# Scale-and-add over 16.8 MB arrays: y whole in SBUF and two large stores, in place of pooled chunks of 16 rows

## The chip, the cores and the metric

The kernel runs on one core of one Trainium2 chip. The metric is the device time of one execution in microseconds (us). The kernel before takes 123.67 us (median of 4 runs, 123.56 to 123.85). Its profiled execution has a span of 122.0 us. The measured time is about 1.7 us more than the span, because the two have different end points.

## The reference

```python
B, S, D = 1024, 16, 512                # bfloat16
x = normal(B, S, D) * 0.05
y = normal(B, S, D) * 0.05
gamma = 1e-4 * normal(D) * 0.05
def reference(x, y, gamma):
    return x + gamma * y
```

There are 16384 rows of 512 elements, 1 KB each. They are spread over 128 partitions, so each partition holds 128 consecutive rows, 128 KB of each array. x and y must be read and the result written: 3 x 16.78 = 50.33 MB.

## The kernel before

The rows are worked in chunks of 16 (the last two of 8). x and y pass through pools of 5 and 6 buffers. SP issues the loads of x, ACT those of y, and GpSimd the stores. These are three separate DMA queues. VectorE multiplies y by gamma in place and then adds x. A scheduler orders the VectorE instructions.

```python
MAIN_CHUNK = 16
TAIL_CHUNKS = [8, 8]
X_BUFS = 5
Y_BUFS = 6
...   # gamma is broadcast to 128 partitions by a matmul with ones; a pad aligns the pools to 16 KB
    for cs in chunks:
        xt = x_pool.tile([P, max_chunk, D], xf.dtype, tag="xt")
        yt = y_pool.tile([P, max_chunk, D], yf.dtype, tag="yt")
        nc.sync.dma_start(out=xt[:, :cs, :], in_=xv[:, r0 : r0 + cs, :])
        nc.scalar.dma_start(out=yt[:, :cs, :], in_=yv[:, r0 : r0 + cs, :])
        nc.vector.tensor_tensor(out=yt[:, :cs, :], in0=yt[:, :cs, :],
            in1=gamma_sb[:, None, :].to_broadcast([P, cs, D]), op=mybir.AluOpType.mult)
        nc.vector.tensor_tensor(out=yt[:, :cs, :], in0=xt[:, :cs, :], in1=yt[:, :cs, :],
            op=mybir.AluOpType.add)
        nc.gpsimd.dma_start(out=ov[:, r0 : r0 + cs, :], in_=yt[:, :cs, :])
        r0 += cs
```

Of the kernel before, what the change touches and what calls it, by code (L numbers as in the profile page):

```python
# [1 line left out]

# [4 lines left out]

MAIN_CHUNK = 16
TAIL_CHUNKS = [8, 8]
X_BUFS = 5  # L10
Y_BUFS = 6
SBUF_ALIGN = 16384
SLOT_ROUND = 32


def _chunk_schedule(n_per_part: int) -> list[int]:
    tail = [c for c in TAIL_CHUNKS if c < MAIN_CHUNK]
    rem = n_per_part - sum(tail)
    if rem < 0:
        return [1] * n_per_part  # L20
    chunks = []
    while rem >= MAIN_CHUNK:
        chunks.append(MAIN_CHUNK)
        rem -= MAIN_CHUNK
    if rem > 0:
        chunks.append(rem)
    chunks.extend(tail)
    assert sum(chunks) == n_per_part, (chunks, n_per_part)
    return chunks


def _round_up(v: int, m: int) -> int:
    return ((v + m - 1) // m) * m


@with_exitstack
def kernel(
    ctx: ExitStack,
    tc: tile.TileContext,
    x: bass.AP,  # L40
    y: bass.AP,
    gamma: bass.AP,
    out: bass.AP,
):
    nc = tc.nc
    P = nc.NUM_PARTITIONS

    xf = x.flatten_outer_dims()
    yf = y.flatten_outer_dims()
    of = out.flatten_outer_dims()  # L50
    N, D = xf.shape
    assert N % P == 0, (N, P)
    n_per_part = N // P
    gdt = gamma.dtype

    xv = xf.rearrange("(p n) d -> p n d", p=P)
    yv = yf.rearrange("(p n) d -> p n d", p=P)
    ov = of.rearrange("(p n) d -> p n d", p=P)

    chunks = _chunk_schedule(n_per_part)  # L60
    max_chunk = max(chunks)

    const_pool = ctx.enter_context(tc.tile_pool(name="const", bufs=1))
    gamma_row = const_pool.tile([1, D], gdt)
    ones_row = const_pool.tile([1, P], gdt)
    gamma_sb = const_pool.tile([P, D], gdt)
    used = nc.sbuf_base
    used = _round_up(used, SLOT_ROUND)
    for nbytes in (D * mybir.dt.size(gdt), P * mybir.dt.size(gdt), D * mybir.dt.size(gdt)):
        used += _round_up(nbytes, SLOT_ROUND)  # L70
    pad_bytes = (-used) % SBUF_ALIGN
    pad_sb = None
    if pad_bytes > 0:
        pad_sb = const_pool.tile([P, pad_bytes], mybir.dt.uint8)

    x_pool = ctx.enter_context(tc.tile_pool(name="xio", bufs=X_BUFS))
    y_pool = ctx.enter_context(tc.tile_pool(name="yio", bufs=Y_BUFS))
    psum_pool = ctx.enter_context(tc.tile_pool(name="psum", bufs=1, space=bass.MemoryType.PSUM))

    nc.gpsimd.dma_start(out=gamma_row[:], in_=gamma.unsqueeze(0))  # L80
    nc.vector.memset(ones_row[:], 1.0)  # L81
    if pad_sb is not None:
        nc.vector.memset(pad_sb[:, 0:64], 0)  # L83
    gamma_ps = psum_pool.tile([P, D], mybir.dt.float32)
    nc.tensor.matmul(gamma_ps[:], ones_row[:], gamma_row[:], start=True, stop=True)  # L85
    nc.vector.tensor_copy(out=gamma_sb[:], in_=gamma_ps[:])  # L86

    r0 = 0
    for cs in chunks:
        xt = x_pool.tile([P, max_chunk, D], xf.dtype, tag="xt")  # L90
        yt = y_pool.tile([P, max_chunk, D], yf.dtype, tag="yt")
        nc.sync.dma_start(out=xt[:, :cs, :], in_=xv[:, r0 : r0 + cs, :])
        nc.scalar.dma_start(out=yt[:, :cs, :], in_=yv[:, r0 : r0 + cs, :])  # L93
        nc.vector.tensor_tensor(  # L94
            out=yt[:, :cs, :],
            in0=yt[:, :cs, :],
            in1=gamma_sb[:, None, :].to_broadcast([P, cs, D]),
            op=mybir.AluOpType.mult,
        )
        nc.vector.tensor_tensor(  # L100
            out=yt[:, :cs, :],
            in0=xt[:, :cs, :],
            in1=yt[:, :cs, :],
            op=mybir.AluOpType.add,
        )
        nc.gpsimd.dma_start(out=ov[:, r0 : r0 + cs, :], in_=yt[:, :cs, :])  # L106
        r0 += cs
    assert r0 == n_per_part


# [1 line left out]
_INS = ['x', 'y', 'gamma']  # L112
_OUTS = [((1024, 16, 512), 'bfloat16')]


# [23 lines left out]
```

## Time and profile before

| what | value | where it is read |
|---|---|---|
| time, span | 123.67 us, 122.0 us | runs, page |
| bytes | 50.33 MB, 412 GB/s over the span | page, DMA queues |
| DMA engines busy | 32.7 + 32.7 + 32.2 = 97.6% | page, DMA queues |
| VectorE busy | 71.1 us, 58% | page, busy time |
| one VectorE operation | 4.42 us for 8192 columns, 2.29 for 4096 | groups by shape |

These lines are from the page of the kernel before. "DMA" is the busy share of the 16 engines in tenths, for 40 equal slices of 3.05 us; "GB/s" is what they moved. The three lines below are the DMA queues with packets, MB and share of the 16 engines' span: q1 is SP's queue, q10 is ACT's, q0 is GpSimd's.

```profile
...
DMA  4999999999999999999999999999999999999993
GB/s 118 424 435 430 430 430 430 430 349 435 430 430 435 435 440 430 430 430 430 430 440 435 430 430 430 430 430 430 430 397 454 413 430 419 464 430 430 397 427 126
...
q10 hardware_dynamic: 1296, 16.78, 32.7%
q1 hardware_dynamic: 1296, 16.78, 32.7%
q0 software_dynamic: 1328, 16.78, 32.2%
...
```

Every slice but the first and the last is at 9, the highest digit. The rate is about 430 GB/s both while only loads run and while stores are mixed in. The Trainium skill ("DMA: Bandwidth & Descriptors", section "Where 436 GB/s comes from") gives 435 GB/s as the ceiling of the ports; this trace agrees within 1 to 2%. So the kernel is bound by the DMA engines, and its bytes alone need 117 us at 430 GB/s.

The next lines are groups of VectorE instructions of the kernel before, with shapes kept apart: count, busy us, mean ns of one, then the idle time before them and what ended it.

```profile
...
L94 DVE TENSOR_TENSOR yt<-yt,gamma_sb 128x8192 bf16<-128x8192 bf16 x7 | 31.0, 4423 | 33.4 <-DMA yt<-in_y_dram 33.4
L100 DVE TENSOR_TENSOR yt<-xt,yt 128x8192 bf16<-128x8192 bf16 x7 | 30.7, 4419 | 0.0
...
L94 DVE TENSOR_TENSOR yt<-yt,gamma_sb 128x4096 bf16<-128x4096 bf16 x2 | 4.6, 2287 | 2.0 <-DMA yt<-in_y_dram 2.0
...
```

Here is the beginning of its timeline: start, duration, engine, line, operation, and in brackets the idle time before it.

```profile
...
13.06 4.42 DVE L94 TENSOR_TENSOR yt<-yt,gamma_sb 128x8192 bf16<-128x8192 bf16 x1 [3.82 <-DMA yt<-in_y_dram]
17.52 4.42 DVE L100 TENSOR_TENSOR yt<-xt,yt 128x8192 bf16<-128x8192 bf16 x1
22.26 0.55 POOL L106 DMA_DIRECT2D out_dram<-yt  x1 [20.38 <-DVE yt L100]
...
36.19 4.42 DVE L94 TENSOR_TENSOR yt<-yt,gamma_sb 128x8192 bf16<-128x8192 bf16 x1 [9.04 <-DMA yt<-in_y_dram]
...
```

VectorE waits for y again and again (33.4 us before the large multiplies). The first store is issued at 22.26 us, so from then on stores and loads share the engines.

### The profile page before, as it was taken

What the parts mean: (1) busy time and instruction counts of PE and PEld (TensorE: products, weight loads), DVE (VectorE), ACT (ScalarE), POOL (GpSimd) and SP (SyncE); (2) the same over time, 40 slices, a digit from 0 to 9 for tenths busy, and PEclk for the clock granted to TensorE, in tenths of its full rate; (3) what the DMA queues carried; (4) which work ended last, traced back from release to release, by engine and by line L of the source; (5) the groups of instructions that cost most, each with busy time, mean ns of one, the idle gap of its engine ahead of it and who ended that gap; (6) DMA issues with size and microseconds to landing.
All of it is one profiled execution on the core that took longest, in us unless ns stands there. A gap on an engine that the chain in (4) does not pass through costs nothing.

```text
span 122.0 us, 123 instructions
## 1 busy us (share of the span) xinstructions
PE 0.6 (0%) x1; PEld 0.1 (0%) x1; DVE 71.1 (58%) x21; POOL 5.6 (5%) x14
## 2 busy tenths in 40 slices
PE   0010000000000000000000000000000000000000
PEld 0000000000000000000000000000000000000000
DVE  0010799780019999950079995940019999859600
POOL 2000000100000010100000011000000010100300
DMA  4999999999999999999999999999999999999993
GB/s 118 424 435 430 430 430 430 430 349 435 430 430 435 435 440 430 430 430 430 430 440 435 430 430 430 430 430 430 430 397 454 413 430 419 464 430 430 397 427 126
DMA packets 3920, 50.33 MB, mean 412 GB/s; under 512 B 464, under 2 KB 464, under 8 KB 464
## 3 DMA queue, kind: packets, MB, share of 16 engines
q10 hardware_dynamic: 1296, 16.78, 32.7%
q1 hardware_dynamic: 1296, 16.78, 32.7%
q0 software_dynamic: 1328, 16.78, 32.2%
HBM read 33.56 MB, written 16.78 MB: 412 GB/s over the span
## 4 chain that ended last, share of the span: by engine, by line
DMA 66%; issue 15%; DVE 11%; POOL 1%; POOLq 0%; DVEq 0%; ACTq 0%
DMA yt<-in_y_dram 50%; DMA out_dram<-yt 16%; DVE yt L100 7%; DVE yt L94 4%; POOL out_dram L106 1%; POOLq L134 0%; DVEq L94 0%; POOLq L106 0%; ACTq L93 0%; DVEq L100 0%
## 5 line engine op out<-in xcount | busy, mean ns | idle before, releaser
L94 DVE TENSOR_TENSOR yt<-yt,gamma_sb 128x8192 bf16<-128x8192 bf16 (+1 forms) x9 | 35.5, 3949 | 35.5 <-DMA yt<-in_y_dram 35.5
L100 DVE TENSOR_TENSOR yt<-xt,yt 128x8192 bf16<-128x8192 bf16 (+1 forms) x9 | 35.2, 3944 | 0.0
L106 POOL DMA_DIRECT2D out_dram<-yt x9 | 4.8, 533 | 109.1 <-DVE yt L100 109.1
L86 DVE CAST gamma_sb<-gamma_ps 128x512 bf16<-128x512 f32 x1 | 0.7, 690 | 7.5 <-PE gamma_ps L85 7.5
L80 POOL DMA_DIRECT2D gamma_row<-in_gamma_dram x1 | 0.6, 618 | 0.8 <-POOLq L123 0.8
L81 DVE MEMSET ones_row<- 1x128 bf16 x1 | 0.2, 165 | 0.8 <-PEq L123 0.8
L85 PE MATMUL gamma_ps<-gamma_row,ones_row 1*128 1x512 bf16 x1 | 0.6, 577 | 7.9 <-DMA gamma_row<-in_gamma_dram 7.9
L123 POOL MEMSET const-float32-0.0<- 128x1 f32 x1 | 0.1, 98 | 0.2 <-issue 0.2
L123 POOL MEMSET const-bfloat16-1.0<- 128x1 bf16 x1 | 0.1, 102 | 0.0
L85 PEld LDWEIGHTS <-ones_row 1*128 1x128 bf16 x1 | 0.1, 101 | 1.0 <-DVE pad_sb L83 1.0
L123 POOL MEMSET const-float32-1.0<- 128x1 f32 x1 | 0.1, 98 | 0.0
L123 POOL MEMSET const-uint8-127<- 128x1 uint8 x1 | 0.1, 98 | 0.0
L83 DVE MEMSET pad_sb<- 128x16 uint32 x1 | 0.1, 72 | 0.0
## 6 DMA issues: line engine op xcount, KB each, us to landing
yt<-in_y_dram ACTq DMA_DIRECT2D x7, 2048.0 KB, 45.5
xt<-in_x_dram SPq DMA_DIRECT2D x7, 2048.0 KB, 45.4
out_dram<-yt POOLq DMA_DIRECT2D x7, 2048.0 KB, 19.1
xt<-in_x_dram SPq DMA_DIRECT2D x2, 1024.0 KB, 44.4
yt<-in_y_dram ACTq DMA_DIRECT2D x2, 1024.0 KB, 32.7
out_dram<-yt POOLq DMA_DIRECT2D x2, 1024.0 KB, 5.5
gamma_row<-in_gamma_dram POOLq DMA_DIRECT2D x1, 1.0 KB, 6.6
```

The costliest lines, as they stand in the source:

```text
L80: nc.gpsimd.dma_start(out=gamma_row[:], in_=gamma.unsqueeze(0))
L81: nc.vector.memset(ones_row[:], 1.0)
L83: nc.vector.memset(pad_sb[:, 0:64], 0)
L85: nc.tensor.matmul(gamma_ps[:], ones_row[:], gamma_row[:], start=True, stop=True)
L86: nc.vector.tensor_copy(out=gamma_sb[:], in_=gamma_ps[:])
L94: nc.vector.tensor_tensor(out=yt[:, :cs, :], in0=yt[:, :cs, :], in1=gamma_sb[:, None, :].to_broadcast([P, cs, D]), op=mybir.AluOpType.mult,)
L100: nc.vector.tensor_tensor(out=yt[:, :cs, :], in0=xt[:, :cs, :], in1=yt[:, :cs, :], op=mybir.AluOpType.add,)
L106: nc.gpsimd.dma_start(out=ov[:, r0 : r0 + cs, :], in_=yt[:, :cs, :])
L123: nc = _bacc.Bacc("TRN2", target_bir_lowering=False, num_devices=1)
```

## The change

The intent is fewer and larger transfers. y stays whole in SBUF (128 KB per partition), the result replaces it, and all loads of y can be issued at once. x passes through two slots of 32 rows. Two stores of 64 rows (64 KB per partition) close the program: the first on SP's queue, behind the last load of x, the second on ACT's queue, behind the last load of y. The order is the program's own; no scheduler moves anything.

```diff
-MAIN_CHUNK = 16
-TAIL_CHUNKS = [8, 8]
-X_BUFS = 5
-Y_BUFS = 6
+PIECE = 32
+X_SLOTS = 2
+STORE = 64
 ...                                  # the 16 KB alignment pad goes too
+    y_sb = y_pool.tile([P, rows, D], dt)
+    ctx.enter_context(tc.manual_schedule())
+    for c in range(n_pieces):
+        r = slice(c * PIECE, (c + 1) * PIECE)
+        xt = x_pool.tile([P, PIECE, D], dt, tag="xt")
+        yt = y_sb[:, r, :]
+        nc.sync.dma_start(out=xt[:], in_=xv[:, r, :])
+        nc.scalar.dma_start(out=yt, in_=yv[:, r, :])
 ...                                  # the same multiply and add, on 32 rows
-        nc.gpsimd.dma_start(out=ov[:, r0 : r0 + cs, :], in_=yt[:, :cs, :])
+    for c in range(rows // STORE):
+        r = slice(c * STORE, (c + 1) * STORE)
+        eng = nc.sync if c % 2 == 0 else nc.scalar
+        eng.dma_start(out=ov[:, r, :], in_=y_sb[:, r, :])
```

Below, piece 0 to 3 are the four pieces of 32 rows, and x2, y3 and so on are their loads.

More of the change, by code (lines that the diff above doesn't have):

```diff
@@ L6 @@
 from concourse._compat import with_exitstack
-MAIN_CHUNK = 16
-TAIL_CHUNKS = [8, 8]
-X_BUFS = 5
-Y_BUFS = 6
-SBUF_ALIGN = 16384
-SLOT_ROUND = 32
-def _chunk_schedule(n_per_part: int) -> list[int]:
-    tail = [c for c in TAIL_CHUNKS if c < MAIN_CHUNK]
-    rem = n_per_part - sum(tail)
-    if rem < 0:
-        return [1] * n_per_part
-    chunks = []
-    while rem >= MAIN_CHUNK:
-        chunks.append(MAIN_CHUNK)
-        rem -= MAIN_CHUNK
-    if rem > 0:
-        chunks.append(rem)
-    chunks.extend(tail)
-    assert sum(chunks) == n_per_part, (chunks, n_per_part)
-    return chunks
-def _round_up(v: int, m: int) -> int:
-    return ((v + m - 1) // m) * m
+PIECE = 32
+X_SLOTS = 2
+STORE = 64
 @with_exitstack
@@ L51 @@
     N, D = xf.shape
-    assert N % P == 0, (N, P)
-    n_per_part = N // P
-    gdt = gamma.dtype
+    rows = N // P
+    n_pieces = rows // PIECE
+    dt = xf.dtype
     xv = xf.rearrange("(p n) d -> p n d", p=P)
@@ L58 @@
     ov = of.rearrange("(p n) d -> p n d", p=P)
-    chunks = _chunk_schedule(n_per_part)
-    max_chunk = max(chunks)
     const_pool = ctx.enter_context(tc.tile_pool(name="const", bufs=1))
-    gamma_row = const_pool.tile([1, D], gdt)
-    ones_row = const_pool.tile([1, P], gdt)
-    gamma_sb = const_pool.tile([P, D], gdt)
-    used = nc.sbuf_base
-    used = _round_up(used, SLOT_ROUND)
-    for nbytes in (D * mybir.dt.size(gdt), P * mybir.dt.size(gdt), D * mybir.dt.size(gdt)):
-        used += _round_up(nbytes, SLOT_ROUND)
-    pad_bytes = (-used) % SBUF_ALIGN
-    pad_sb = None
-    if pad_bytes > 0:
-        pad_sb = const_pool.tile([P, pad_bytes], mybir.dt.uint8)
-    x_pool = ctx.enter_context(tc.tile_pool(name="xio", bufs=X_BUFS))
-    y_pool = ctx.enter_context(tc.tile_pool(name="yio", bufs=Y_BUFS))
+    gamma_row = const_pool.tile([1, D], dt)
+    ones_row = const_pool.tile([1, P], dt)
+    gamma_sb = const_pool.tile([P, D], dt)
     psum_pool = ctx.enter_context(tc.tile_pool(name="psum", bufs=1, space=bass.MemoryType.PSUM))
@@ L81 @@
     nc.vector.memset(ones_row[:], 1.0)
-    if pad_sb is not None:
-        nc.vector.memset(pad_sb[:, 0:64], 0)
     gamma_ps = psum_pool.tile([P, D], mybir.dt.float32)
@@ L86 @@
     nc.vector.tensor_copy(out=gamma_sb[:], in_=gamma_ps[:])
-    r0 = 0
-    for cs in chunks:
-        xt = x_pool.tile([P, max_chunk, D], xf.dtype, tag="xt")
-        yt = y_pool.tile([P, max_chunk, D], yf.dtype, tag="yt")
-        nc.sync.dma_start(out=xt[:, :cs, :], in_=xv[:, r0 : r0 + cs, :])
-        nc.scalar.dma_start(out=yt[:, :cs, :], in_=yv[:, r0 : r0 + cs, :])
+    y_pool = ctx.enter_context(tc.tile_pool(name="y", bufs=1))
+    x_pool = ctx.enter_context(tc.tile_pool(name="x", bufs=X_SLOTS))
+    y_sb = y_pool.tile([P, rows, D], dt)
[6 more added lines that the diff above has]
+        nc.scalar.dma_start(out=yt, in_=yv[:, r, :])
         nc.vector.tensor_tensor(
-            out=yt[:, :cs, :],
-            in0=yt[:, :cs, :],
-            in1=gamma_sb[:, None, :].to_broadcast([P, cs, D]),
+            out=yt,
+            in0=yt,
+            in1=gamma_sb[:, None, :].to_broadcast([P, PIECE, D]),
             op=mybir.AluOpType.mult,
         )
-        nc.vector.tensor_tensor(
-            out=yt[:, :cs, :],
-            in0=xt[:, :cs, :],
-            in1=yt[:, :cs, :],
-            op=mybir.AluOpType.add,
-        )
-        nc.gpsimd.dma_start(out=ov[:, r0 : r0 + cs, :], in_=yt[:, :cs, :])
-        r0 += cs
-    assert r0 == n_per_part
+        nc.vector.tensor_tensor(out=yt, in0=xt[:], in1=yt, op=mybir.AluOpType.add)
+    for c in range(rows // STORE):
+        r = slice(c * STORE, (c + 1) * STORE)
+        eng = nc.sync if c % 2 == 0 else nc.scalar
+        eng.dma_start(out=ov[:, r, :], in_=y_sb[:, r, :])
 _INS = ['x', 'y', 'gamma']
```

## The prediction

> **What bounds the kernel now.** The 16 DMA engines. The page's DMA row is 9 (of 10) in every slice except the first and the last, and the three DMA queues add up to 32.7 + 32.7 + 32.2 = 97.6% of the engines' span. 50.33 MB move at 424 to 435 GB/s in nearly all slices, loads alone (first 22 us) or mixed with stores. The Trainium skill, "DMA: Bandwidth & Descriptors", section "Where 436 GB/s comes from", gives a ceiling of 435 GB/s for the ports; this trace agrees. VectorE is busy 58% and hidden. At 430 GB/s the bytes alone need 117.0 us of the 122.0 us span. About 5 us are left: about 2.2 us before the first bytes flow (first slice: 118 GB/s), the last landing and the end, and small dips (349 and 397 GB/s slices).
>
> **What the change does.** Bytes are the same. Loads go from 2 MB to 4 MB, stores from nine (issued by GpSimd, spread over the run) to two of 8 MB (SP and ACT), both late. So the run becomes a load phase, then a store phase. The question is only whether the DMA engines ever run dry.
>
> **Estimate, from the trace's numbers** (430 GB/s; start 2.2 us; landing about 1.1 us after the last byte: the first 4 MB pair landed at 13.0 us). VectorE took 4.42 us for 8192 columns and 2.28 us for 4096, so 16384 columns should take 8.7 us, and a piece (multiply and add) 17.4 us. A piece's loads, 8.39 MB, take 19.5 us: VectorE is a little quicker than the DMA and keeps up.
> - x0, y0 land at 22.8; piece 0 done at 40.3; x2 is issued then. x1's bytes end at 41.2, so the SP queue is short of work for about 0.6 us, but y2 is already queued on ACT and fills the engines.
> - x1, y1 land at 42.3; piece 1 done at 59.8; x3 and the first store are issued then, before x2's bytes end (61.3).
> - Loads end at about 80.3; piece 2 is done at 78.9, piece 3 at about 98.
> - The first store, behind x3 in SP's queue, streams from 80 to about 99.7. The second store is issued at 98.3 and flows from about 99.6. Almost no gap, but the margin is under 1 us.
> - Last byte at about 119.5, span about 121.5.
>
> The removed GpSimd issues (9 x 0.53 us) are off the critical path: worth nothing. Lost may be: a gap of 0 to 3 us before the second store, and a slower store-only phase (slices after the last load showed 430, 397 and 427 GB/s; 3% over 40 us is 1.2 us). The skill's section "Issuing engines are not separate DMA queues" says that the issuing engine does not matter; so I expect one queue alone to fill the 16 engines. This trace does not show that.
>
> **Prediction.** Measured time is about 1.7 us over the span: 123.4 us, range 121.9 to 126.2. Faster by over 2%: 0.04; within 2%: 0.85; slower: 0.11.
>
> **What would show it.** DMA row 9 throughout; bandwidth about 430 in both phases; VectorE operations of 8.7 us; last VectorE operation ending near 98 us; the second store issued within 1 us of the first store's last byte; chain of waits: loads, then the last multiply and add, then the second store.
>
> **What would make it wrong.** A store-only phase on a single queue well below 430 GB/s (slower); 4 MB loads landing unevenly, so that piece 3 ends after the first store (slower by that gap); removal of the 16 KB alignment pad slowing transfers; or a phase of pure reads or pure writes running above 435 GB/s (faster).

## The result and the profile after

The changed kernel takes 123.38 us (median of 4 runs, 123.06 to 123.58) against 123.67 us. The ratio is 0.9973, with a 95% interval of 0.9955 to 0.9991: the same within 2%, though a 0.3% gain is clear of noise. Ratios here and below are the mean time of one kernel's fast runs over that of the other's of the same rounds, so they are not quite the ratios of the medians quoted.

The same lines of the page of the changed kernel, in slices of 3.03 us:

```profile
...
DMA  6898989899999999999999999897997799777970
GB/s 173 367 497 378 486 378 486 378 486 400 465 400 465 400 465 400 465 400 465 400 465 400 465 400 465 346 519 346 562 475 346 346 627 411 346 346 346 692 346 0
...
q1 hardware_dynamic: 720, 25.17, 49.0%
q10 hardware_dynamic: 720, 25.17, 48.3%
...
```

The engines are busy 97.3%, against 97.6% before. Here the DMA row shows digits from 7 to 9, not 9 throughout. That is no idle time: the page counts a whole packet, its bytes and its duration, in the slice in which it starts, and packets are now 32 and 64 KB. When the packet records are spread over the time that they really took, every slice but the first and the last is full to within 1%, in both kernels. GpSimd's queue now carries gamma alone. The packets fell from 3920 to 1472 (without those under 512 B, from 3456 to 1280).

The groups of VectorE operations, shapes kept apart:

```profile
...
L60 DVE TENSOR_TENSOR y_sb<-y_sb,gamma_sb 128x16384 bf16<-128x16384 bf16 x4 | 34.8, 8692 | 15.6 <-DMA y_sb<-in_y_dram 15.6
L66 DVE TENSOR_TENSOR y_sb<-xt,y_sb 128x16384 bf16<-128x16384 bf16 x4 | 34.8, 8691 | 0.1
...
```

One operation on 16384 columns takes 8.69 us (8.7 was predicted). The timeline of the changed kernel from the first load's landing on:

```profile
...
22.90 8.69 DVE L60 TENSOR_TENSOR y_sb<-y_sb,gamma_sb 128x16384 bf16<-128x16384 bf16 x1 [11.10 <-DMA y_sb<-in_y_dram]
31.62 8.69 DVE L66 TENSOR_TENSOR y_sb<-xt,y_sb 128x16384 bf16<-128x16384 bf16 x1
42.27 8.69 DVE L60 TENSOR_TENSOR y_sb<-y_sb,gamma_sb 128x16384 bf16<-128x16384 bf16 x1 [1.96 <-DMA y_sb<-in_y_dram]
51.00 8.69 DVE L66 TENSOR_TENSOR y_sb<-xt,y_sb 128x16384 bf16<-128x16384 bf16 x1
60.09 0.42 SPq L70 DMA_DIRECT2D out_dram<-y_sb  x1
60.10 8.69 DVE L60 TENSOR_TENSOR y_sb<-y_sb,gamma_sb 128x16384 bf16<-128x16384 bf16 x1 [0.41 <-DMA y_sb<-in_y_dram]
68.83 8.69 DVE L66 TENSOR_TENSOR y_sb<-xt,y_sb 128x16384 bf16<-128x16384 bf16 x1
79.61 8.69 DVE L60 TENSOR_TENSOR y_sb<-y_sb,gamma_sb 128x16384 bf16<-128x16384 bf16 x1 [2.09 <-DMA y_sb<-in_y_dram]
88.33 8.69 DVE L66 TENSOR_TENSOR y_sb<-xt,y_sb 128x16384 bf16<-128x16384 bf16 x1
97.05 0.35 ACTq L70 DMA_DIRECT2D out_dram<-y_sb  x1
...
```

Each piece starts when its y lands (22.90, 42.27, 60.10, 79.61 us) and takes 17.4 us. The last one ends at 97.02 us, and the second store is issued at 97.05. The chain that ended last, by line, in the view of the chain:

```profile
...
by line: DMA y_sb<-in_y_dram 33.9%; DVE y_sb L60 21.5%; DVE y_sb L66 21.5%; another core or an unknown queue 2.0%; ACTq L59 0.3%; issue 0.2%
...
```

This chain puts 43% of the span on VectorE. It lists one way back from the end, not what bounds the kernel: the packet records say that the engines were never dry while VectorE worked. The first experiment tests which reading is right. (The chain also does not list the second store, which ends the program at 120.2 us.)

The trace records each packet with its size and duration. I used them for an account of the span. A packet of 8, 16, 32 and 64 KB takes 0.309, 0.611, 1.213 and 2.418 us (medians) on one engine. Twice the time of one size is 7 to 9 ns more than the time of the next size, so by my estimate each packet costs about 8 ns besides its bytes. "Packets" below is count times median over 16 engines. "Start stall" is what packets in the first 5 us took beyond their median, "other" is such excess later plus the time in which engines had no packet, and "end" runs from the end of the last packet to the end of the span. All values are us; one execution each.

```
kernel        first  packets  start stall  other    end   = span
before         1.73   117.48         0.59   0.67   1.58   122.05
changed        1.75   116.32         0.65   1.08   1.48   121.29
tiny_compute   1.77   116.32         0.70   1.01   1.39   121.19
late8          1.74   116.32         0.65   8.01   1.40   128.12
one_store      1.77   116.32         0.63  18.11   1.34   138.16
four_stores    1.74   116.45         0.68   1.21   1.66   121.75
p16            1.75   117.31         0.56   0.52   1.42   121.56
p8             1.74   118.66         0.73   0.30   1.46   122.88
swap           1.75   116.32         0.62   2.97   1.46   123.11
pool_stores    1.74   116.32         0.66  14.91   1.41   135.03
pool_late      1.73   116.38         0.70   0.21   1.48   120.51
sp_three       1.73   116.38         0.73   1.04   1.48   121.37
sp_three_l8    1.74   117.86         0.58   0.70   1.57   122.44
one_slot       1.74   116.32         0.68  23.98   1.40   144.12
```

Two things moved between the first two rows: the packets cost 1.16 us less (136 fewer on each engine, at about 8 ns each), and "other" costs about 0.4 us more. Of the 1.08 us "other" after the change, 0.53 us are slow packets between 75 and 80 us, where the last loads hand over to the first store, and 0.34 us are slow first packets of the second store (from 99.8 us on). Of the 0.67 us before, 0.54 us are slow packets that started between 25 and 30 us, most of them just before the first store, issued at 22.26 us, sent its first packet at 27.17 us. The profiled execution of the changed kernel is the fastest of its four (their spans are 121.3, 121.5, 121.7 and 121.8 us), so the account overstates the gain by a few tenths.

### The profile page after: what moved, and what is told of

The parts are those of the page before. It is cut to its first block, busy times and chain, and to the rows that moved or that the text cites. A ratio compares the mean times of both kernels' runs of the same rounds, so it can differ in the third digit from the quotient of the medians.

```text
span 121.3 us, 77 instructions
## 1 busy us (share of the span) xinstructions
PE 0.6 (0%) x1; PEld 0.1 (0%) x1; DVE 70.4 (58%) x10; POOL 0.8 (1%) x5
## 2 busy tenths in 40 slices
DMA packets 1472, 50.33 MB, mean 415 GB/s; under 512 B 192, under 2 KB 192, under 8 KB 192
## 4 chain that ended last, share of the span: by engine, by line
DVE 43%; DMA 34%; another core or an unknown queue 2%; ACTq 0%; issue 0%
DMA y_sb<-in_y_dram 34%; DVE y_sb L60 22%; DVE y_sb L66 21%; ACTq L59 0%
## 5 line engine op out<-in xcount | busy, mean ns | idle before, releaser
L60 DVE TENSOR_TENSOR y_sb<-y_sb,gamma_sb 128x16384 bf16<-128x16384 bf16 x4 | 34.8, 8692 | 15.6 <-DMA y_sb<-in_y_dram 15.6
L66 DVE TENSOR_TENSOR y_sb<-xt,y_sb 128x16384 bf16<-128x16384 bf16 x4 | 34.8, 8691 | 0.1
L47 PE MATMUL gamma_ps<-gamma_row,ones_row 1*128 1x512 bf16 x1 | 0.6, 581 | 10.5 <-DMA gamma_row<-in_gamma_dram 10.5
```

The source lines that it names most:

```text
L47: nc.tensor.matmul(gamma_ps[:], ones_row[:], gamma_row[:], start=True, stop=True)
L60: nc.vector.tensor_tensor(out=yt, in0=yt, in1=gamma_sb[:, None, :].to_broadcast([P, PIECE, D]), op=mybir.AluOpType.mult,)
L66: nc.vector.tensor_tensor(out=yt, in0=xt[:], in1=yt, op=mybir.AluOpType.add)
```

## The experiments

The theories: A, the DMA engines are the limit and VectorE is hidden, so that only a dry queue costs time. B, VectorE's chain sets the time. A2, the small gain comes from larger packets. C, it comes from loading first and storing after. D, it comes from leaving GpSimd's queue. P, formed after pool_stores failed both A and D: a store's place in the queues matters. All edits are against the changed kernel, and all results are correct unless said otherwise. The changed kernel itself was not run again in these later rounds, which took chips 7, 4 and 5. So a difference from it is read from the two ratios to the kernel before; by their intervals it is uncertain by about 0.3 us.

### tiny_compute: VectorE's work taken away

```diff
-        nc.vector.tensor_tensor(out=yt, in0=yt, in1=gamma_sb[:, None, :]..., op=mult)
-        nc.vector.tensor_tensor(out=yt, in0=xt[:], in1=yt, op=add)
+        nc.vector.tensor_tensor(out=yt[:, 0:1, :], in0=xt[:, 0:1, :], in1=yt[:, 0:1, :], op=add)
```

> Wrong result on purpose: no multiply, and the add works on 1 of a piece's 32 rows, so VectorE's work falls from 70.4 us to about 3 us and all waits stay. Theory A (the 16 DMA engines are never dry, VectorE is hidden): the time stays within 0.6 us of the changed kernel's 123.4 us, still about 0.997 of before. Theory B (the chain through VectorE, which the page puts at 43% of the span, sets the time): several us faster, 118 us or less.

Measured: 122.97 us, ratio 0.9936 (0.9920 to 0.9953), wrong result. These are lines of its page:

```profile
...
DVE  0002000100000000000010000001000000000000
...
DMA  6898989898989898989898989997997799779970
...
```

VectorE is idle, the DMA row is as full as in the changed kernel, and the time fell by about 0.4 us (under 0.8 us by the intervals). B falls: 67.8 us of VectorE work cost no more than that. In this run the second store was issued at 82.16 us, well before its first packet (87.64 us), and its first packets show none of the 0.34 us of slowness. (The profiled execution itself, in the account above, is only 0.1 us shorter than that of the changed kernel: its engines ended within 0.8 us of each other, against 0.4 us, and that of the changed kernel is its fastest.)

### late8: VectorE 8.7 us later at the end

```diff
+        if c == n_pieces - 1:     # ones_sb holds 1.0
+            nc.vector.tensor_tensor(out=yt, in0=yt, in1=ones_sb[:, None, :]..., op=mult)
```

> One more pass of VectorE over the last piece (a multiply by ones, 8.7 us, the result stays right), so the second store is issued 8.7 us later, at about 105.8 us. Theory A with the margin I read (the first store's last byte at about 99.8 to 100.3, the second was issued at 97.05 and a store needs about 1.2 us to flow): the queue stands dry for 8.7 minus 1.5 to 2.0 us, so 6.7 to 7.2 us slower, 130.1 to 130.6 us, with a hole of about 7 us in the DMA row before the second store. If VectorE already set the time (B): the full 8.7 us slower, 132.1 us.

Measured: 129.81 us, ratio 1.0489, 6.4 us over the changed kernel and just under the range expected. The end of its timeline, then the DMA and GB/s rows of its page (slices of 3.2 us):

```profile
...
88.86 8.69 DVE L68 TENSOR_TENSOR y_sb<-xt,y_sb 128x16384 bf16<-128x16384 bf16 x1
97.59 8.69 DVE L70 TENSOR_TENSOR y_sb<-y_sb,ones_sb 128x16384 bf16<-128x16384 bf16 x1
106.31 0.35 ACTq L79 DMA_DIRECT2D out_dram<-y_sb  x1
...
```

```profile
...
DMA  5979979989899899899799899997997007997790
GB/s 164 491 328 491 481 338 491 440 379 491 389 430 491 368 450 491 348 471 481 338 491 440 379 491 327 532 450 327 512 471 327 0 0 327 471 512 327 327 655 0
...
```

The hole stands in the slices from 99.2 us on (two zeros in the GB/s row). By the packets, the engines waited about 7 us for the second store; its first packet went out at 107.17 us, 0.86 us after its issue (1.2 us was expected). So VectorE is hidden, but only by about 2 us at one place: the last piece against the first store. A second multiply over that piece alone costs 6.4 us, three quarters of its length.

### one_store and four_stores: the number of stores

```diff
-STORE = 64
+STORE = 128        # one_store;  four_stores has STORE = 32
```

> One store of 128 rows in place of two of 64. Theory A: nothing is left to stream from the end of the loads (about 80.5 us) until piece 3 is done at 97.05 plus 1.2 us to flow, so a hole of about 17.5 us in the DMA row, span about 139 us, time about 141 us. If the number of stores in itself mattered and not the hole: about 123 us.

Measured: 139.96 us, ratio 1.1309. The DMA row of its page, slices of 3.45 us:

```profile
...
DMA  5999989999998999999899900000797979779790
...
```

The hole is 17.7 us by the packets (17.5 expected). Once the loads are in, nothing is left to move until piece 3 is done. It is the first store, covering the last VectorE work, that makes two stores cost no more than nine.

> Four stores of 32 rows in place of two of 64; SP has stores 0 and 2, ACT 1 and 3. The queues have work earlier and more evenly, but theory A says they were never dry, so it stays within 0.5 us of the changed kernel; store packets halve to 32 KB, which by the two packet durations in the trace (2.418 and 2 x 1.213 us) costs 0.13 us. If the late second store had cost time (a gap of 1 us or more before it), it is 1 us faster or more.

Measured: 123.55 us, ratio 0.9981 (0.9967 to 0.9996). No difference from the changed kernel can be told, as A said.

### p16 and p8: smaller packets

```diff
-        nc.sync.dma_start(out=xt[:], in_=xv[:, r, :])
-        nc.scalar.dma_start(out=yt, in_=yv[:, r, :])
+        for k in range(0, PIECE, 16):     # 8 in p8
+            q = slice(c * PIECE + k, c * PIECE + k + 16)
+            nc.sync.dma_start(out=xt[:, k : k + 16, :], in_=xv[:, q, :])
+            nc.scalar.dma_start(out=y_sb[:, q, :], in_=yv[:, q, :])
 ...                                      # the stores are cut the same way
```

> The changed kernel with every transfer cut so that one packet holds 16 rows (16 KB) in place of 32 or 64; order, VectorE work and slots are the same. Theory A2 (the gain comes from larger packets; the trace has 0.611 us for a packet of 16 KB, 1.213 for 32 KB, 2.418 for 64 KB per engine): packets need 192 x 0.611 = 117.3 us in place of 64 x 1.213 + 16 x 2.418 = 116.3 us, so about 1.0 us slower than the changed kernel, 124.3 us, slower than before by 0.5 us. Theory C (the gain comes from loading first and storing after, packets don't matter): stays at 123.4 us, ratio 0.997.

> The same with 8 rows (8 KB) per packet. A2: 384 packets of 0.309 us per engine are 118.7 us, so 2.3 us over the changed kernel, about 125.7 us, ratio to before 1.015. C: 123.4 us, ratio 0.997. If the many short transfers stall a queue[...], the DMA row shows holes and it is slower still.

Measured: p16 122.99 us (122.71 to 123.70), ratio 0.9944 (0.9920 to 0.9969); p8 124.58 us, ratio 1.0062. p16 missed both expectations: it is not slower than the changed kernel. p8 lies between its two (1.015 and 0.997). The experiment was not clean. Cutting the stores also let piece 2 be stored at 77.5 us instead of with piece 3, and the slow packets around 75 to 80 us shrank from 0.53 to 0.27 us. The account shows the packets costing 0.99 us more and "other" 0.56 us less. From p16 to p8 only the size changed: 1.6 us more, where the packet durations give 1.35 us. So A2 holds in direction, and what offsets it needed a cleaner run (sp_three_l8). Nor does the gain of the change need larger packets: p16's packets cost nearly what those of the kernel before cost (117.31 and 117.48 us), and it is still 0.6% faster than that kernel. So C, the order, is not excluded; no run tests it by itself.

### swap: the first store behind y3, the second behind x3

```diff
-        eng = nc.sync if c % 2 == 0 else nc.scalar
+        eng = nc.scalar if c % 2 == 0 else nc.sync
```

> The first store on ACT's queue behind y3, the second on SP's behind x3. In the changed kernel the packets just before the first store (77.5 to 79.5 us) and the first ones of the second store took 0.3 to 0.6 us longer than the rest, by the trace. If that is because SP's queue alone has work there, both queues having work until about 84 us takes it away: up to 0.4 us faster, 123.0 us. x3 then lands about 3 us later, still before its add at 88.3 us, so nothing is lost. If it comes with any change from loads to stores: no difference, within 0.2 us.

Measured: 124.07 us (123.56 to 124.89), ratio 1.0015 (0.9993 to 1.0036). A miss: slower by 0.4% than the changed kernel, in the other direction than expected. Three lines of its timeline (the profiled execution is the slowest of the six):

```profile
...
59.76 0.37 ACTq L70 DMA_DIRECT2D out_dram<-y_sb  x1
...
81.40 8.69 DVE L60 TENSOR_TENSOR y_sb<-y_sb,gamma_sb 128x16384 bf16<-128x16384 bf16 x1 [3.66 <-DMA y_sb<-in_y_dram]
...
98.85 0.35 SPq L70 DMA_DIRECT2D out_dram<-y_sb  x1
...
```

Piece 3 starts at 81.40 us instead of 79.61, so the second store is issued 1.8 us later. But that is not where the time went: its first packet flows at 99.75 us, as in the changed kernel (99.76). By the records of the landings, 15 of y3's 16 completions came by 78.65 us and the last at 81.38 us: one engine finished its part of the load 2.7 us after the others, about the length of one 64 KB store packet (2.418 us). The first store had queued up right behind y3 and shared the engines with x3 too (x3 landed at 86.3 us instead of 81.3). In the changed kernel the first store sits behind x3, the load that is needed last, and neither happens. In this execution 1.5 us more than in the changed kernel are lost at the very end, where the engines run out at different times, 119.25 to 121.66 us, against 119.45 to 119.81 us. That a store packet held the completion back, and that this is why one engine ended late, was not tested.

### pool_stores: both stores on GpSimd's queue

```diff
-        eng = nc.sync if c % 2 == 0 else nc.scalar
+        eng = nc.gpsimd
```

> Both stores issued by GpSimd, as before the change, nothing else. Theory A: the issuing engine does not matter, within 0.3 us of the changed kernel, ratio 0.997. Theory D (the small gain comes from leaving GpSimd's software queue): back to 123.7 us, ratio 1.000 or more.

Measured: 136.78 us, ratio 1.1044, 13.4 us over the changed kernel. Neither theory had that. The DMA row of its page (slices of 3.38 us), and lines of its timeline:

```profile
...
DMA  5999899998999899999997999899940007797790
...
```

```profile
...
59.87 0.55 POOL L70 DMA_DIRECT2D out_dram<-y_sb  x1 [58.00 <-DVE y_sb L66]
...
95.26 8.69 DVE L60 TENSOR_TENSOR y_sb<-y_sb,gamma_sb 128x16384 bf16<-128x16384 bf16 x1 [17.65 <-DMA y_sb<-in_y_dram]
103.99 8.69 DVE L66 TENSOR_TENSOR y_sb<-xt,y_sb 128x16384 bf16<-128x16384 bf16 x1
112.97 0.53 POOL L70 DMA_DIRECT2D out_dram<-y_sb  x1 [52.55 <-DVE y_sb L66]
...
```

The first store is issued at 59.87 us, as in the changed kernel (60.09). But on a queue of its own it does not stand behind x3. It starts at 64.8 us and competes with x3 and y3. (Why it took 4.9 us from issue to first packet is not shown; in the kernel before the first store took 4.9 us too.) Between 74 and 84 us the three queues started 32, 34 and 33 packets: they take turns by packets. Put in sequence by their start and end times, the packets of each engine go strictly in turn: store, x, y. The Trainium skill says so too ("DMA: Bandwidth & Descriptors", section "Queues, rings and completion order": each engine goes round the queues that have work, a packet at a time); this run agrees, for what the trace records as packets. A store packet is 64 KB and a load packet 32 KB, so the store took half of the bytes. y3 landed at 95.2 us instead of 79.6, piece 3 was done at 112.7, and by 102 us everything else had been moved. The engines then waited 13.6 us for the second store.

### pool_late: GpSimd's queue again, but later

```diff
-    for c in range(rows // STORE):
-        r = slice(c * STORE, (c + 1) * STORE)
-        eng = nc.sync if c % 2 == 0 else nc.scalar
-        eng.dma_start(out=ov[:, r, :], in_=y_sb[:, r, :])
+    for a, b in [(64, 96), (0, 64), (96, 128)]:
+        nc.gpsimd.dma_start(out=ov[:, a:b, :], in_=y_sb[:, a:b, :])
```

> All stores again on GpSimd, but as three, with piece 2's rows (64 to 96) first, then rows 0 to 64, then rows 96 to 128. GpSimd's queue works in order, so nothing is stored before piece 2 is done at 77.5 us, when x3 and y3 have nearly landed; the store is still on a third queue, not behind x3. Theory P (pool_stores lost 13 us because its first store flowed from 62 us on in competition with x3 and y3, and the second, which needs piece 3, came late): the loss is gone, x3 and y3 land 1 to 3 us later than in the changed kernel, stores of 12.6 MB cover the time until piece 3 is done, 123 to 124.5 us. Theory D (stores from GpSimd's software queue are slow in themselves): about 136 us again.

Measured: 122.31 us (122.29 to 122.33), ratio 0.9896 (0.9880 to 0.9911): 14.5 us faster than pool_stores on the same queue, 1.0% faster than before, and the fastest of all. It is even below the range that I expected, since x3 and y3 landed no later than in the changed kernel (80.7 and 79.4 us, against 81.3 and 79.6). Lines of its page, then of its timeline:

```profile
...
DMA  6898989898989898989898989999998899888983
...
q0 software_dynamic: 464, 16.78, 32.2%
...
```

```profile
...
77.75 1.07 POOL L68 DMA_DIRECT2D out_dram<-y_sb  x2 [75.88 <-DVE y_sb L66]
79.44 8.69 DVE L60 TENSOR_TENSOR y_sb<-y_sb,gamma_sb 128x16384 bf16<-128x16384 bf16 x1 [2.00 <-DMA y_sb<-in_y_dram]
88.17 8.69 DVE L66 TENSOR_TENSOR y_sb<-xt,y_sb 128x16384 bf16<-128x16384 bf16 x1
97.16 0.53 POOL L68 DMA_DIRECT2D out_dram<-y_sb  x1 [18.33 <-DVE y_sb L66]
...
```

GpSimd's queue waits for piece 2 first (77.75 us). The first store packet flows at 79.96 us, when x3's last packets are already running, so piece 3 starts on time (79.44 us). D falls: stores from GpSimd's queue are not slow. P holds: what cost pool_stores 13 us was that the first store flowed beside the last loads. pool_late also cuts the second store in two, but that is not the cure: the changed kernel, with two stores, has no such loss, and sp_three below, with three, is no faster than it. The remaining gain, over the changed kernel, is in the "other" column: 0.21 us in place of 1.08. The slow packets at the handover and at the second store are both gone.

### sp_three and sp_three_l8: all stores on SP's queue; then small load packets alone

```diff
+    for a, b in [(0, 64), (64, 96), (96, 128)]:
+        nc.sync.dma_start(out=ov[:, a:b, :], in_=y_sb[:, a:b, :])
 ...                        # replaces the two stores; sp_three_l8 also cuts each load into four of 8 rows
```

> Three stores, all on SP's queue behind x3: rows 0 to 64, 64 to 96 and 96 to 128. Piece 2 can be stored at 77.5 us, so 12.6 MB of stores are queued and last until about 110 us; the last store waits for piece 3 (97 us) without a gap, and no store competes with x3 or y3. Theory A with the 0.4 us that the late second store cost (tiny_compute against the changed kernel): about 0.3 to 0.4 us faster than the changed kernel, 123.0 us, ratio 0.994. If several stores or one queue alone cost time: 123.4 us or more.

> sp_three with each load of 32 rows cut to four of 8 rows (8 KB packets in place of 32 KB); stores untouched, and piece 3 has 12 us of slack here, so the confusion of p16 and p8 (which also let piece 2 be stored early) is gone. A2 (packets): 33.55 MB in packets of 8 KB take 256 x 0.309 = 79.1 us per engine in place of 64 x 1.213 = 77.6 us, so 1.5 us slower than sp_three, 124.5 us. Rival (packet size does not matter): same as sp_three within 0.3 us.

Measured: sp_three 123.15 us, ratio 0.9963 (0.9950 to 0.9975), not to be told from the changed kernel (0.9973); 0.994 was expected. The slow packets of the last store are gone, as expected, but those at the handover were 0.72 us in place of 0.53. sp_three_l8: 124.06 us, ratio 1.0038 (1.0026 to 1.0051), 0.9 us more than sp_three of the same rounds. The size of the packets matters, though less than the 1.5 us expected. (Cutting the loads also makes 32 transfers of 8; the durations of the packets, and not the run's time, tell the two apart.) The account shows where the rest went: the packets cost 1.48 us more, but the slow packets at the handover vanished (0.07 us in place of 0.72), and after small losses all along the way 0.5 us of the start stall and of "other" came back.

### one_slot: one slot for x

```diff
-X_SLOTS = 2
+X_SLOTS = 1
```

> One slot for x in place of two, so a load of x waits for the add before it. Theory A (nothing but dry queues costs time): y runs ahead and is in by about 60 us; x1 is issued at 40.3 and lands at about 61 us, x2 is issued at about 70, x3 at about 91 us, each alone for about 10 us, with about 10 us of nothing before each: holes of about 20 us in all, about 142 us (139 to 145). If y's running ahead hid it: below 128 us.

Measured: 145.76 us, ratio 1.1792; slightly above the range given. The DMA row of its page (slices of 3.6 us) and VectorE's wait for x (total us, times, longest):

```profile
...
DMA  5999999999999999600589500499969696969690
...
```

```profile
...
DVE y_sb L66 <- DMA xt<-in_x_dram: 21.0, 3, 12.6
...
```

The two holes before x2 and x3 are about 10.5 us each, as expected. The account has 2.6 us of slow packets besides, after the holes and at the handover. The second slot of x is worth 22 us here; that y is whole doesn't replace it.

## Why the prediction was right

The predicted time was 123.4 us, and 123.38 us were measured. Step by step:

- **The DMA engines bound both kernels.** Shown for the changed kernel: tiny_compute took away nearly all VectorE work for about 0.4 us. For the kernel before it rests on its profile alone, whose DMA row is full; no run edits that kernel. The prediction's sign "DMA row 9 throughout" did not come (7 to 9), for the reason given with the page; the packet records are full.
- **A VectorE pass of 8.7 us, and the timetable of pieces.** Shown: 8.69 us. Piece 1 was done at 59.69 us (59.8 predicted), piece 2 at 77.52 (78.9), piece 3 at 97.02 (98), and the loads ended at 81.0 us (80.3). The last packet ended at 119.8 us (119.5).
- **The margin before the second store.** It was predicted to be issued at 98.3 us and to flow from 99.6 us, almost without a gap. It was issued at 97.05, its first packet went at 99.76, and those packets were slow by 0.34 us. late8 puts the margin at about 2 us, wider than the "under 1 us" predicted, because piece 3 was done about 1 us earlier. So the sign "issued within 1 us of the first store's last byte" did not come either: that byte went at 100.32 us, 3.3 us after the issue.
- **The rate.** The prediction took 430 GB/s for both kernels, and so gave the larger packets nothing. They are worth 1.16 us by the packet durations; sp_three_l8 shows the effect in time, at 0.9 us for a cut of the loads from 32 to 8 KB. The prediction also gave nothing for the handover from loads to stores (0.53 us) or the slow start of the second store (0.34 us). These mis-sized terms have opposite signs and nearly cancel, so the total is closer than its parts deserve: that it is right to 0.02 us is luck.
- **"The issuing engine does not matter."** For one queue's rate this held: the store phase was full, from SP and then from ACT alone. As a general statement it was wrong (the page says only that all issuing engines share the same 16 DMA engines), and pool_stores shows it: the same stores on GpSimd's queue cost 13.4 us. The timetable rested on the first store standing "behind x3, in SP's queue"; the prediction named that place and did not say that the result hung on it.
- **The chain of waits** was predicted to end with the second store; the view of the chain stopped at the last add.
- **The removed alignment pad** was named as a risk. p16, which has no pad, shows the same 0.611 us for a packet of 16 KB as the kernel before, which has it; the pad was not tested by itself.

What stays open: why packets run slow at the handover. In the packet records it is 0.5 to 0.7 us with 32 KB loads in tiny_compute, late8, sp_three, swap and four_stores, where a store was queued while the last loads ran, 0.27 us with 16 KB, and at most 0.08 us with 8 KB, in one_store (no store queued then) and in pool_late (first store issued only 2.2 us before it flowed). It is not GpSimd's queue that avoids it: in pool_stores the packets from 60 to 65 us, most of them loads just before its first store's first packet, lost 0.89 us. No run separates the causes.

## What to carry to other kernels

When the DMA engines are full, a change of buffers, pieces or stores can gain only what the engines lose, here 1 to 2 us of 122, so first add up bytes, packets and gaps. What such a change can lose is much more: a queue that holds a store back behind the last load is worth 13 us here, a second slot 22 us, and a store that covers the last piece's work 17 us. Place stores so that they flow after the loads which the last computation needs, and so that enough of them are queued to cover it. pool_late does that and beats both kernels (122.31 us); sp_three does it too and gains nothing clear over the changed kernel (123.15 us). What sets them apart is the slow packets at the handover, and their cause is open.

## What the Trainium skill lacked or had wrong

- "DMA: Bandwidth & Descriptors", section "Issuing engines are not separate DMA queues": it says that issuing from several engines only saves the sequencer's time. Neither it nor the page's account of the queues draws the consequence that the choice of the queue decides what a transfer has to wait behind: moving two stores to another queue took the time from 123.38 to 136.78 us (pool_stores), and holding them back there gave 122.31 us (pool_late).
- The same page, section "Queues, rings and completion order", has the turn by packets. It lacks the consequence that larger packets take a larger share: with 64 KB store packets against two queues of 32 KB load packets, 32, 34 and 33 packets went out in 10 us, and y3 landed at 95.2 us in place of 79.6.
- The same page, section "Where 436 GB/s comes from", says that for transfers between HBM and SBUF the HBM side (about 358 GB/s) binds. With one core at work the runs show about 430 GB/s for loads and for stores. (The page's own single-core measurement, 425 GB/s, agrees with the runs; by its note on that measurement, about 358 GB/s is each core's share when both cores stream.)
- The same page, section "Why small descriptors are slow (HBM only)", works its example for a descriptor of 256 bytes. It has no figures for large ones, where the runs still show a cost, about 8 ns a packet by the estimate above: packets of 8, 16, 32 and 64 KB took 0.309, 0.611, 1.213 and 2.418 us, so 26.5 to 27.1 GB/s per engine, up to 2% of the time of a kernel that only moves data.
- No page has the slow packets at a handover from loads to stores: 0.5 to 0.9 us in most runs, none in pool_late.
